# Gated delta rule and softplus MLP on one core: four of six base inverses in 32 lanes instead of two joined 16s, beta from SP and ACT, tile fills as scheduled items, another order

## The chip, the cores and the metric

The kernel runs on one core of one Trainium2 chip. The metric is the device time of one execution in microseconds. TensorE is called PE, VectorE DVE, ScalarE ACT, GpSimd POOL, and SyncE SP; SP, ACT and POOL issue the DMAs. DVE and POOL work on SBUF tiles of 128 partitions; results of PE lie in PSUM and are evicted by DVE or ACT.

## The reference

Two parts follow each other. The first is a gated delta rule over 4 batches, 8 heads, 768 positions and 48 features:

```python
k_n = k / (np.linalg.norm(k, axis=-1, keepdims=True) + 1e-06)
for t in range(S):
    y[:, :, t] = g[:, :, t] * einsum('bhd,bhde->bhe', q[:, :, t], state)
    v_old = einsum('bhde,bhd->bhe', state, k_n[:, :, t])
    state = state + beta[t] * einsum('bhd,bhe->bhde', k_n[:, :, t], v[:, :, t] - v_old)
```

The second takes y as a matrix of 3072 tokens by 384 features and computes `softplus(y @ w_in) @ w_out`, with 2048 hidden features.

## The kernel before

**Chunks and pairs.** The positions are cut into 12 chunks of 64. Within a chunk the recurrence is turned into matmuls; from chunk to chunk only the state is carried. Two chunks make a pair (pair 0 has chunks 0 and 1, pair 5 has chunks 10 and 11). Per chunk the kernel loads k, q, v and g (each in two DMAs of 192 KB, L249 and L271), scales k by its norm (L327 `kmul`, or a plain cast for pair 0), transposes k and q on PE (L345, L388), forms the products k k^T and k q^T (L503), evicts them (`kkc`; `mask`, L518), and runs the chain of the recurrence.

**The inverse of a pair.** Each chunk and head needs the inverse of a unit lower triangular matrix of 64 x 64, made of beta and k k^T. It is built in layers:

- The *base* is computed by DVE or POOL for all heads of both chunks at once: one partition holds one block. The strictly lower entries are transposed into lanes (L604 `kd1`, L611 `ln`), the tile `tt` is cleared (L619), its diagonal set to beta (L621), the entries scaled by beta into `nn` (L629 `prep`). Then `step` j, of two instructions (L639 a product into `tmp`, L646 an add into `tt`), adds row j's share to all rows below. Each partition holds two blocks of 16 x 16 (an upper and a lower one of a block of 32), so there are 15 steps.
- The two blocks of 16 are joined to one of 32, the *inner join*: `cv` (L228) and `tn` (L667, a transpose) bring the upper block back, `xmm` (L707, 32 matmuls a chunk) and `tmm` (L732, 32 a chunk) multiply it with the entries between the blocks, `xs` evicts between them and `thi` after them.
- `c16` casts `tt` to 16 bits, `t32` (L686) transposes it back, `tlo` writes it into `te` (used by `umm`, L855) and `to` (used by `zmm`, L770), scaled by masks.
- The outer join, from 32 to 64, is inside the recurrence: `zmm` and `z` (L779) make a tile z, and `zu` (L878) applies it.

nn, tt, tmp-like tiles have few buffers (nn 1, tt 1, tmp 2), so pairs follow each other there. Norms of pairs 2 to 5 take a power on POOL (`pow`, L566) after a square on ACT (L545) and a reduction on DVE (L549); pairs 0 and 1 take a square root on ACT.

**The chain of a chunk.** `ks` and `qs` (L813) multiply the state with k and q; `w` (L847) is v minus that; `umm`, the copy `u1`, `zu`, the copy `u2`; then `ymm` (L928) and `y` (L943, times g) give the output, and `smm` (L898) and `s` (L913) the next state. y is transposed (L962) into `xt`.

**The MLP** fills PE between: groups g1 (L992, into `h`, then softplus on ACT, L1004, into `ga`) and g2 (L1019, into `o`, copied by L218 or L220 and stored, L1039). A g1 group has 3 matmuls of 512 columns or 6 of 256, a g2 group 4 of 384. The weights come by eight DMAs from POOL (L297). `warm` items (L1064) are three matmuls on the identity whose result nobody reads.

**What sets the order.** Each piece of work is an item with the engines that may run it, the items it needs, and the buffers it uses. One list written into the kernel, `_ORDER`, names engine and number of every item: `P707` would put item 707 on PE. Engines work through their own part of the list in order, so an instruction that waits holds all behind it on its engine. A tile takes the first free buffer of its ring when its first item is emitted:

```python
for word in table.split():
    en, no = word[0], int(word[1:])
    it = self.items[no]
    ...
    for b in it.bufs:
        if b.ap is None:
            b.slot = b.ring.free.pop(0)
    it.fn(en)
```

Ahead of the list stand fixed instructions: identity, masks, the padding of kn and qn, the constant halves of the tiles te and z (L205, L212), and eight DMAs for beta from POOL (L175).

Of the kernel before, what the change touches and what calls it, by code (L numbers as in the profile page):

```python
# [74 lines left out]
def kernel(  # L75
# [20 lines left out]
    RAW = (0,)  # L96
    ON_ACT = (0, 1)
    IDLE = 24
# [34 lines left out]
    r_nv = ring("nv", 3, [P, 32], F32)  # L133
# [5 lines left out]
    r_mt = ring("mt", 10, [P, H, C], F16)  # L139
# [12 lines left out]
    r_w = ring("w16", 4, [P, H, D], F16)  # L152
# [15 lines left out]
    for r in range(2):  # L168
        for hf in range(2):
            l0 = 32 * (2 * r + hf)  # L170
            src = beta[2 * r : 2 * r + 2].rearrange(
                "p h (c l r) -> (p h) l c r", l=2, r=64
            )
            for cl in range(2):
                nc.gpsimd.dma_start(  # L175
                    out=beta_l[l0 + 16 * cl : l0 + 16 * cl + 16],
                    in_=src[:, cl, :, 32 * hf : 32 * hf + 32],
                )
# [25 lines left out]
    for t in r_te.tiles:  # L204
        nc.vector.tensor_copy(t[:, :, HC:], id64[:, 1, None, :].broadcast_to([P, U, HC]))  # L205
# [23 lines left out]

    def f16ps(ap):  # L230
        return ap.bitcast(F16)
# [6 lines left out]


# [296 lines left out]
    nv_of, td_of, z_of = {}, {}, {}  # L536
    root_last = [None]
# [38 lines left out]
    def inverse(cc, kk, kk_it, kkd, kd_it, nv, nv_it):  # L576
# [11 lines left out]
        if raw:  # L588
            bl_it = add("lbeta", tag, "D", lbeta, deps=[nv_it], bufs=[nv, nl, bl])
            bb = [bl]  # L590
        else:
            bl_it, bb = None, []
# [5 lines left out]
        if not raw:  # L598
# [4 lines left out]
            def kd1(en):  # L603
# [12 lines left out]
        en0 = "D" if first else "G"  # L616
        eng = ENG[en0]
        prev = add("clear", tag, "D" if first else "GD",
                   lambda en: ENG[en].memset(tt.ap, 0.0), bufs=[tt])  # L619
        prev = add("diag", tag, en0,  # L620
                   lambda en: eng.tensor_copy(  # L621
                       tt.ap.rearrange("p b i j -> p b (i j)")[:, :, ::17],
                       bl_ap().rearrange("p (b i) -> p b i", b=2),
                   ),
                   deps=[prev, bl_it], bufs=[tt] + bb)

        def prep(en, b):
            r = slice(16 * b, 16 * b + 16)
            eng.tensor_tensor(  # L629
                nn.ap[:, b].rearrange("p i (t e) -> p i t e", e=2),  # L630
                ln.ap[:, 8 * b : 8 * b + 8, r].rearrange("p t i e -> p i t e"),
                bl_ap()[:, r, None, None].broadcast_to([P, 16, 8, 2]),
                ALU.mult,
            )

        def step(en, j):
            n, w = 15 - j, j + 1
            t = tmp.ap[:, : 2 * n * w].rearrange("p (b i c) -> p b i c", b=2, c=w)
            eng.tensor_tensor(  # L639
                t,  # L640
                nn.ap[:, :, j + 1 :, j : j + 1].broadcast_to([P, 2, n, w]),
                tt.ap[:, :, j : j + 1, :w].broadcast_to([P, 2, n, w]),
                ALU.mult,
            )
            rows = tt.ap[:, :, j + 1 :, :w]
            eng.tensor_tensor(rows, rows, t, ALU.add)  # L646

        for b in range(2):
            prev = add("prep", f"{tag}.{b}", en0, lambda en, b=b: prep(en, b),
                       deps=[l1, prev, bl_it], bufs=[ln, nn] + bb)  # L650
        for j in range(15):
            prev = add("step", f"{tag}.{j}", en0, lambda en, j=j: step(en, j),
                       deps=[prev], bufs=[nn, tt, tmp], size=2 * (15 - j) * (j + 1))

        tw, tv, td, tn = Buf(r_tw), Buf(r_tv), Buf(r_td), Buf(r_tn)
# [517 lines left out]
```

## Time and profile before

| | |
|---|---|
| three runs | 254.86, 257.12, 260.44 us; median 257.12 |
| the profiled execution | 255.46 us, span 253.6 us, mean granted clock 0.966 |
| busy in the span | PE 93%, DVE 61%, ACT 60%, POOL 50% |
| costliest groups | softplus (L1004) 56.3 us, g1 (L992) 73.3, g2 (L1019) 70.3, POOL steps (L639, L646) 30.1 and 29.4, pow (L566) 21.8 |
| DMA | 27.56 MB in all, near 180 GB/s until 63 us |

The span is from the first to the last instruction of the profiled execution; the time has a little around it. Busy shares count an engine as busy while an instruction of its own is running; matmuls overlap, so PE's share is no measure of how well it is used. The page's digits show tenths of 40 equal slices of 6.34 us.

### The profile page before, as it was taken

Reading aid. Unit: us, or ns where it says so; the run is one execution under the profiler, and the core shown is the slowest. Engines: PE = TensorE matmul, PEld = TensorE weight load, DVE = VectorE, ACT = ScalarE, POOL = GpSimd, SP = SyncE. Lnnn points to the kernel's source line nnn. Section 1 sums busy time; section 2 is a strip of 40 time slices with the busy share of each in tenths; the row PEclk is TensorE's granted clock in tenths of the full one; section 3 lists DMA queues with packets and bytes.
Section 4 is the critical chain, followed back from the end, with each engine's and each line's share of the span. In section 5 each row is a group of like instructions: output and inputs, shape, how many; then the busy total and the mean of one; then the engine's idle time right before and its main releaser. Section 6 shows DMA issues by size and latency. Waiting matters only on the chain.

```text
span 253.6 us, 11355 instructions
## 1 busy us (share of the span) xinstructions
PE 236.9 (93%) x5040; PEld 160.5 (63%) x5040; DVE 153.7 (61%) x311; ACT 153.0 (60%) x285; POOL 127.1 (50%) x227
## 2 busy tenths in 40 slices
PE   7976588998989999999999999999999999999993
PEld 3543577676766765666766767755676565777751
DVE  7789888775893699759697588523843315313000
ACT  3557777686866579973777675456453475223530
POOL 8201653978879889988948859884000000000000
PEclk9999757799999999999999999999999999999999
DMA  8999999999990789083943850643024130112113
GB/s 111 198 181 178 178 179 180 186 195 176 176 153 6 173 180 157 4 200 83 156 98 84 170 99 22 124 83 80 3 66 93 23 80 0 34 32 48 34 47 78
DMA packets 86192, 27.56 MB, mean 109 GB/s; under 512 B 76288, under 2 KB 86144, under 8 KB 86144
## 3 DMA queue, kind: packets, MB, share of 16 engines
q1 hardware_dynamic: 80096, 23.21, 50.2%
q0 software_dynamic: 3968, 3.25, 8.2%
q10 hardware_dynamic: 2080, 0.39, 1.2%
q8 instruction: 39, 0.64, 1.2%
q14 instruction: 9, 0.07, 0.1%
HBM read 25.26 MB, written 4.72 MB: 118 GB/s over the span
## 4 chain that ended last, share of the span: by engine, by line
PE 76%; DVE 9%; DMA 4%; issue 3%; SPq 2%; ACT 2%; POOL 2%; ACTq 0%; DVEq 0%; POOLq 0%
PE h L992 25%; PE o L1019 23%; PE d L813 4%; DMA beta_l<-in_beta_dram 3%; PE d L855 3%; PE d L732 3%; PE d L770 3%; PE d L878 2%; PE d L928 2%; PE d L503 2%; PE d L707 2%; PE d L898 2%; PE d L388 2%; PE d L345 2%; POOL beta_l L175 2%
## 5 line engine op out<-in xcount | busy, mean ns | idle before, releaser
L1004 ACT ACTIVATE ga<-h 128x512 f16<-128x512 f32 x96 | 56.3, 598 | 33.4 <-PE h L992 27.6
L992 PE MATMUL h<-xt,w_in 128*128 128x512 f16 (+1 forms) x384 | 73.3, 330 | 0.1
L1019 PE MATMUL o<-w_out,ga 128*128 128x384 f16 x384 | 70.3, 326 | 1.4 <-issue 0.7
L1019 PEld LDWEIGHTS <-ga 128*128 128x128 f16 x384 | 35.7, 98 | 23.9 <-issue 1.8
L992 PEld LDWEIGHTS <-w_in 128*128 128x128 f16 x384 | 35.6, 99 | 20.7 <-issue 0.6
L639 POOL TENSOR_TENSOR tmp<-nn,tt 128x30 f32<-128x30 f32 (+7 forms) x75 | 30.1, 401 | 5.6
L646 POOL TENSOR_TENSOR tt<-tt,tmp 128x30 f32<-128x30 f32 (+7 forms) x75 | 29.4, 392 | 5.9
L566 POOL TENSOR_TENSOR nv<-nv,half_c 128x32 f32<-128x32 f32 x4 | 21.8, 5456 | 5.1 <-DVE nv L549 5.1
L218 ACT ACTIVATE kqt<-d 128x1024 f16<-128x1024 f16 (+1 forms) x21 | 18.4, 903 | 7.0 <-PE d L388 6.1
L218 ACT ACTIVATE osb<-o 128x384 f32<-128x384 f32 x18 | 8.8, 489 | 21.5 <-PE o L1019 21.4
L943 DVE TENSOR_TENSOR yg<-d,gf 128x384 f16<-128x384 f32 x24 | 12.8, 553 | 13.6 <-PE d L928 10.2
L1064 PE MATMUL o<-ident 128*128 128x512 f16 x72 | 19.3, 411 | 1.4 <-POOL ident masks.py:199 1.4
L847 DVE TENSOR_TENSOR w<-vf,d 128x384 f16<-128x384 f32 x22 | 11.3, 549 | 12.0 <-PE d L813 10.8
L218 ACT ACTIVATE u<-d 128x384 f16<-128x384 f32 x31 | 14.3, 491 | 7.1 <-PE d L878 3.3
L218 ACT ACTIVATE kk<-d 128x256 f16<-128x256 f32 (+1 forms) x34 | 12.8, 413 | 7.8 <-PE d L503 6.4
L518 DVE TENSOR_TENSOR mt<-d,mask 128x256 f16<-128x256 f32 x40 | 15.5, 418 | 3.2 <-PE d L503 1.9
L220 DVE CAST u<-d 128x384 f16<-128x384 f32 x17 | 9.1, 549 | 13.1 <-PE d L878 11.6
L813 PEld LDWEIGHTS <-kqt 48*64 48x64 f16 x704 | 13.3, 108 | 5.5 <-issue 5.3
L220 DVE COPY osb<-o 128x384 f32<-128x384 f32 x6 | 3.3, 556 | 21.6 <-PE o L1019 21.6
L813 PE MATMUL d<-s,kqt 48*64 48x48 f16 x704 | 16.4, 188 | 0.0
L545 ACT ACTIVATE ksq<-kf 128x768 f32<-128x768 f32 x12 | 10.1, 843 | 7.6 <-DMA kf<-in_k_dram 6.7
L220 POOL CAST tw<-tt 128x256 f16<-128x256 f32 x10 | 5.4, 563 | 16.1 <-DVE tt L646 16.0
(110 smaller groups left out, 380.1 us busy)
## 6 DMA issues: line engine op xcount, KB each, us to landing
qf<-in_q_dram SPq DMA_DIRECT2D x24, 192.0 KB, 5.1
vf<-in_v_dram SPq DMA_DIRECT2D x24, 192.0 KB, 5.2
gf<-in_g_dram SPq DMA_DIRECT2D x24, 192.0 KB, 4.2
out_dram<-osb SPq DMA_DIRECT2D x48, 96.0 KB, 2.4
kf<-in_k_dram SPq DMA_DIRECT2D x22, 192.0 KB, 5.1
w_in<-in_moe_w_in_dram POOLq DMA_DIRECT2D x4, 384.0 KB, 7.5
w_out<-in_moe_w_out_dram POOLq DMA_DIRECT2D x4, 384.0 KB, 12.9
kf<-in_k_dram ACTq DMA_DIRECT2D x2, 192.0 KB, 7.5
```

Of the source, the lines that this page charges most:

```text
L218: nc.scalar.activation(o, x, AF.Copy, scale=float(sign))
L220: ENG[en].tensor_copy(o, x)
L518: nc.vector.tensor_tensor(mt[c][m].ap[:, NP * p : NP * p + NP], gb[m].ap.rearrange("p (n b) -> p n b", n=NP)[:, :, C:], mask[:, None, :].b ...
L566: lambda en: nc.gpsimd.tensor_tensor(nv.ap, nv.ap, half_c, ALU.pow),
L639: eng.tensor_tensor(t, nn.ap[:, :, j + 1 :, j : j + 1].broadcast_to([P, 2, n, w]), tt.ap[:, :, j : j + 1, :w].broadcast_to([P, 2, n, w]), ...
L646: eng.tensor_tensor(rows, rows, t, ALU.add)
L813: nc.tensor.matmul(hd(o.ap)[HALF[r], NP * p + i], kq_of(c)[FEAT[m], 8 * p + 2 * i + r, off : off + C], s0[r].ap[FEAT[m], NP * p + i], **st ...
L943: lambda en, m=m: nc.vector.tensor_tensor(heads(yg.ap, m), hd(yp[m].ap), heads(gf.ap, m), ALU.mult),
L992: nc.tensor.matmul(hp.ap[:, n * b : n * b + n], w_in[:, j, f * P : (f + 1) * P], xt.ap[:, j, t0 : t0 + n], start=(j == 0), stop=(j == 2),)
L1004: lambda en, hp=hp, o=gb: nc.scalar.activation(o.ap, hp.ap, AF.Softplus),
L1019: nc.tensor.matmul(op.ap[:, :DM], b.ap[:, col + c0 : col + c0 + 128], w_out[:, f, :], start=(f == 0), stop=(f == NF - 1),)
L1064: nc.tensor.matmul(wb.ap.rearrange("p (a b) -> p a b", a=4), ident, ident[:, None, :].broadcast_to([P, 4, P]),)
```

## The change

- Pairs 2 to 5 (`WIDE`) compute their base in 32 lanes: one block of 32 x 32 a partition, 31 steps, `tt` and `nn` of 1,024 elements, `tmp` of up to 256. `cv`, `tn`, `xmm`, `xs`, `tmm` and `thi` fall away for them; `tlo` writes all 32 columns. Pairs 0 and 1 stay in two 16s.
- The steps of pairs 1 to 5 may now stand on DVE or POOL item by item (`en0`); the list alternates them inside a pair: of the wide steps 73 stand on DVE and 51 on POOL.
- beta is loaded by eight items, four on SP and four on ACT, instead of eight instructions on POOL ahead of the list.
- The constant halves of te and z are filled by items (`fte`, `fz`) on DVE, ACT and POOL.
- v of chunk 0 is scaled into w directly (`w0`), without the separate `vs`.
- There are 32 `warm` items instead of 24. Rings: nv 2 instead of 3, mt 9 instead of 10, w16 3 instead of 4, tmp 1 instead of 2.
- Five `gate` items on POOL copy one column each of kn, kk and kqt of chunks 0 and 1.
- `_ORDER` is another list, on all engines. Among others the SP list brings q of chunk 1 before that of chunk 0, and v3, k6 and k7 before g1; and POOL scales k of chunks 2 and 3.

The diff without the list, tile sizes and names cut where they repeat:

```diff
+    WIDE = (2, 3, 4, 5)
-    IDLE = 24
+    IDLE = 32
...
-    r_n = ring("nn", 1, [P, 2, 16, 16], F32)
-    r_tmp = ring("tmp", 2, [P, 128], F32)
-    r_t = ring("tt", 1, [P, 2, 16, 16], F32)
+    r_n = ring("nn", 1, [P, HC * HC], F32)
+    r_tmp = ring("tmp", 1, [P, HC * HC // 4], F32)
+    r_t = ring("tt", 1, [P, HC * HC], F32)
...
-            for cl in range(2):
-                nc.gpsimd.dma_start(
-                    out=beta_l[l0 + 16 * cl : l0 + 16 * cl + 16],
-                    in_=src[:, cl, :, 32 * hf : 32 * hf + 32],
-                )
...
-    for t in r_te.tiles:
-        nc.vector.tensor_copy(t[:, :, HC:], id64[:, 1, None, :].broadcast_to([P, U, HC]))
-    for t in r_z.tiles:
-        nc.vector.tensor_copy(t[:, :, :HC], pat[:, None, :].broadcast_to([P, 16, HC]))
+    fill_te = [add("fte", f"f{i}", "DAG", ...) for i, t in enumerate(r_te.tiles)]
+    fill_z = [add("fz", f"f{i}", "DAG", ...) for i, t in enumerate(r_z.tiles)]
...
+                def beta_load(en, r=r, hf=hf, cl=cl):
+                    l0 = 32 * (2 * r + hf) + 16 * cl
+                    src = beta[2 * r, 0, C * cl + 32 * hf :]
+                    ENG[en].dma_start(out=beta_l[l0 : l0 + 16], in_=bass.AP(...))
+                beta_it.append(add("beta", f"{r}{hf}{cl}", "SA", beta_load))
...
-        en0 = "D" if first else "G"
-        eng = ENG[en0]
+        en0 = "D" if first else "DG"
+        wide = cc in WIDE
+        nb, bs = (1, HC) if wide else (2, HC // 2)
...
         def step(en, j):
-            n, w = 15 - j, j + 1
-            t = tmp.ap[:, : 2 * n * w].rearrange("p (b i c) -> p b i c", b=2, c=w)
-            eng.tensor_tensor(
+            n, w = bs - 1 - j, j + 1
+            t = tmp.ap[:, : nb * n * w].rearrange("p (b i c) -> p b i c", b=nb, c=w)
+            nn_, tt_ = n_ap(), t_ap()
+            ENG[en].tensor_tensor(
...
-        for j in range(15):
+        for j in range(bs - 1):
...
-        cv = add("cv", tag, "DG", cvs, deps=[prev], bufs=[tt, tv])
+        cv = None if wide else add("cv", tag, "DG", cvs, deps=[prev], bufs=[tt, tv])
...
-        for cl in range(2):
+        for cl in () if wide else range(2):
             xp = Buf(p_d)
...
-                        en, b.ap[:, :, :16], td.ap[:, :, :16], own[:, x : x + 1]
+                        en, b.ap[:, :, :bs], td.ap[:, :, :bs], own[:, x : x + 1]
...
-            its = [
+            its = lo if wide else [
...
-                a2 = add("w0", f"{c}.{m}", "DGA",
-                         lambda en, m=m, w1=w1: copy(en, w1.ap, heads(vf.ap, m)),
+                a2 = add("w0", f"{c}.{m}", "DG",
+                         lambda en, m=m, w1=w1: ENG[en].tensor_tensor(w1.ap, heads(vf.ap, m), ..., ALU.mult),
...
+    gates = pool.tile([P, 8], F16, name="gates")
+    for x, (it, b) in enumerate(gate_of):
+        add("gate", f"{x}", "G", ..., deps=[it], bufs=[b])
```

More of the change, by code (lines that the diff above doesn't have):

```diff
@@ L228, in scaled @@
             ENG[en].tensor_scalar_mul(o, x, by)
+    fill_te = [
+        add("fte", f"f{i}", "DAG",
+            lambda en, t=t: copy(
+                en, t[:, :, HC:], id64[:, 1, None, :].broadcast_to([P, U, HC])
+            ))
+        for i, t in enumerate(r_te.tiles)
+    ]
+    fill_z = [
+        add("fz", f"f{i}", "DAG",
+            lambda en, t=t: copy(en, t[:, :, :HC], pat[:, None, :].broadcast_to([P, 16, HC])))
+        for i, t in enumerate(r_z.tiles)
+    ]
     def f16ps(ap):
@@ L588, in inverse @@
         if raw:
[L589 removed]
+            bl_it = add("lbeta", tag, "D", lbeta, deps=[nv_it] + beta_it, bufs=[nv, nl, bl])
             bb = [bl]
@@ L820, in chain @@
         vs = None
-        if cc in RAW:
+        if cc in RAW and not first:
             vs = add("vs", f"{c}", "GD",
```

251 lines of the change are left out of this document (145 added, 106 removed).

## The prediction

> **What bounds the kernel now.** I read the page first, then windows, chain, timeline, rows by form, DMA. From the page:
>
> ```profile
> span 253.6 us, 11355 instructions
> PE 236.9 (93%) x5040; PEld 160.5 (63%) x5040; DVE 153.7 (61%) x311; ACT 153.0 (60%) x285; POOL 127.1 (50%) x227
> PE   7976588998989999999999999999999999999993
> DVE  7789888775893699759697588523843315313000
> POOL 8201653978879889988948859884000000000000
> PEclk9999757799999999999999999999999999999999
> ```
>
> From slice 10 (63 us) TensorE is never free, while POOL, which computes the base inverses, is done after slice 28 (178 us). Two windows, and three pieces of the chain of waits (start, length, x matmuls):
>
> ```profile
> 27.90:41.50 13.60, 11.78 (x325) 10.69 (x321) 10.88 (x21) 10.79 (x24) 9.27 (x10) 0.50 1.08 185
> 60.00:249.00 189.00, 187.28 (x4000) 126.38 (x3998) 105.51 (x188) 113.46 (x210) 95.66 (x177) 1.00 0.45 88
> ```
>
> ```profile
> 56.16 0.65 PE o L1064 x3
> 98.00 1.11 PE d L707 x64
> 191.54 0.91 PE d L732 x58
> ```
>
> In the windows the first pair of numbers after the length is PE's busy time: 187.3 of 189 us from 60 to 249, so there any work taken from PE shows in the end, as long as nothing else falls behind. The page's PEclk dips in slices 5 to 8; the first window shows the granted clock 0.50.
>
> How early the inverses are ready is in the timeline: POOL ends the last one (pair 5, chunks 10 and 11) at 173.8, and PE's L770 needs it for chunk 10 at 199.0 and for chunk 11 only at 218.3.
>
> ```profile
> 164.06 0.43 POOL L639 TENSOR_TENSOR tmp<-nn,tt 128x128 f32<-128x128 f32 x1
> 164.56 0.45 POOL L646 TENSOR_TENSOR tt<-tt,tmp 128x128 f32<-128x128 f32 x1
> 170.47 0.24 POOL L639 TENSOR_TENSOR tmp<-nn,tt 128x30 f32<-128x30 f32 x1
> 172.92 0.84 POOL L220 CAST tw<-tt 128x256 f16<-128x256 f32 x2
> 218.27 0.66 PE L770 MATMUL d<-to,kk 64*64 64x32 f16 x32
> ```
>
> **The change, part by part.** *PE.* Pairs 2 to 5 lose L707 and L732: 4 x (1.11 + 1.0) = 8.4 us (58 of 64 of L732 took 0.91). Eight more fills of three 512-column matmuls (L1064) at 0.65 each come back: 5.2. Both lie in dense stretches, the fills at the first three chunks, so I count the net: -3.2 us. If every added fill lay in a PE gap it would be -8.4, if half the removed work was hidden, +1.
>
> *The base inverses.* In 16 lanes a pair takes 15 steps of two instructions over 1,360 elements each way; in 32 lanes 31 steps over 5,456. Rows by form:
>
> ```profile
> L629 POOL TENSOR_TENSOR nn<-ln,beta_l 128x256 f32<-128x256 f16 x10 | 6.0, 619 | 4.6 <-DVE ln L611 3.3 <-DVE nv L570 1.3
> L639 DVE TENSOR_TENSOR tmp<-nn,tt 128x30 f32<-128x30 f32 x2 | 0.4, 197 | 0.1
> L639 DVE TENSOR_TENSOR tmp<-nn,tt 128x126 f32<-128x126 f32 x2 | 0.6, 292 | 0.1
> L629 DVE TENSOR_TENSOR nn<-ln,bl 128x256 f32<-128x256 f16 x2 | 0.8, 422 | 0.0
> L566 POOL TENSOR_TENSOR nv<-nv,half_c 128x32 f32<-128x32 f32 x4 | 21.8, 5456 | 5.1 <-DVE nv L549 5.1
> ```
>
> DVE: 168 ns + 1.0 per element (30, 126 and 256 elements), and 42 between dependent ones. POOL: 190 + 1.9 per element (0.24 for 30, 0.44 for 128; the 256 of L629 at 619 would give 1.7), and 78 between (164.06 + 0.43 to 164.56). The built order puts 73 of the 124 wide steps on DVE, 51 on POOL, alternating inside each pair. They are one chain: each step reads the last, and nn, tt and tmp have one buffer, so pair k+1 begins when pair k is cast.
>
> The chain, from the end of the second step of pair 2 (time S) to the matmul L770 of chunk 11:
> - POOL: 102 x 0.268 + 18,290 x 0.0019 = 62.1
> - DVE: 71 steps, 142 x 0.210 + 25,358 x 0.0010, = 55.2
> - three times clear (1.0), diag (0.2) and prep of 1,024 elements (1.2; the last on POOL 1.9): 7.9; four casts: 5.0 (POOL's two of 256 take 0.84; 1,024 in one on DVE or ACT lie between 1.0 and 1.9, I take 1.0 to 1.1, POOL 1.9)
> - one pow (L566) stands on POOL between two steps of pair 2: 5.4
> - transpose and the two scalings te, to after the last cast: 2.3
>
> That is 138. At each change of pair DVE first has other work: the transpose (1.03), ln (1.05), two w (0.55 each), a copy of o, and a pow that is not fully covered, some 8 in all. Elsewhere POOL's runs (1 to 9.7 us) are as long as what DVE does beside them, so I add nothing. Sum 146; bounds 138 to 156.
>
> *Port.* Beside DVE's wide operation a POOL step can stand still:
>
> ```profile
> 64.85 1.44 DVE L604 SCALAR_TENSOR_TENSOR kkd<-kk,own,kkd 128x1024 f16<-128x1024 f16 x1 [0.98 <-ACT kkd L226]
> 65.29 1.19 POOL L639 TENSOR_TENSOR tmp<-nn,tt 128x78 f32<-128x78 f32 x1
> ```
>
> The next of the same size takes 0.34: 0.85 lost. Two such a pair would cost 7; DVE's wait beside may swallow them; I take 1. [...]
>
> *When S is.* Beta leaves POOL (L175, 4.5 us of issue) for SP and ACT, four each at some 0.7 us; the fills lie before data arrives. This trace has no beta from SP or ACT: the last is issued at about 7, and at the 2.4 to 5.1 us from issue to landing of the page's groups it lands between 9.5 and 12; DVE needs it at 12.3. That saves the 0.8 idle at L585 (0.3 if another 0.5 us passes). The transpose tn ahead of a reduction saves 0.9. So the first pair is 1.6 earlier. But pair 1 waits for POOL, whose queue is now: two k-scalings (1.5 each), the cast of q4, three weight issues (0.8), pow (5.4), a weight issue, prep (1.2), nine steps (8.1).
>
> ```profile
> q1 hardware_dynamic: 80096, 23.21, 50.2%
> q0 software_dynamic: 3968, 3.25, 8.2%
> ```
>
> 50.2% of the span for 23.21 MB is 1.08 us for a 192 KB load, and 8.2% 2.6 us per weight. The second half of q4 is the 28th load: 28 x 1.08 + 2 weights + 2 us start + some 1.5 in which SP waits for a q buffer = 39. Then 0.8 + 2.4 + 5.4 + 0.8 + 1.2 + 8.1 + 1 (POOL's first two steps took 0.84 and 0.86) = 58.7, DVE's six steps to 62. Cast, reduction, y, tn, clear, L604, ln, prep, two steps and three masks follow on DVE: 10. S = 72; 66 if q4 is no brake, 76 if other loads are (below).
>
> *Sum.* S 72 + chain 146 + port 1 = 219 at L770 of chunk 11. PE would get there at about 210: in the new order 179 us of its work lie before it, and 31 us of gaps as in this trace (249 less 217.5 of work at the dense rates 0.65 per group and 0.2 to 0.5 for the small ones). So PE waits some 9 us, spread over the pairs, the 3.2 are lost and 6 more. Behind that point PE has 35 (28 groups L1019, 16 L992 at 0.65, the last two chunks' small ones), a gap of 0.6 as at 246.65 in the timeline, and 4.2 from the last matmul to the end (249.4 to 253.6): 259 to 260. ACT loses some 10 us of evictions off the path; nothing. The gates are five one-column POOL copies; nothing, covered by POOL's waits.
>
> Profiled time is 255.46 for a span of 253.6; 259.5 gives 261.4, +2.3%. The median of the three runs, 257.12, is 0.65% above the profiled one; on that scale 263, and I say **262**.
>
> **Rivals.** (1) PE stays the bound: not slower. If POOL's runs hide DVE's other work and S is 66 to 68, the chain reaches 210 with PE; then only -3.2 counts: span 250.5, 254 on the scale of the median. For it: DVE was free for 2.3 of each 10 us from 30 to 160; against: it gains 56 us of steps and loses some 16 (four tn, five thi, nine copies u, two k-scalings). It decides when S + chain falls under 210. (2) The added fills keep the clock at 1.0 where it was 0.50 (27.9 to 41.5) and the first pair's gain reaches chunk 1: PE regains up to 5 of 11.8, S 62: span 246, 249. Against: the small matmuls there wait for ACT and DVE. (3) Loads come late: the new SP order puts g1 41st, behind k6, k7 and v3 (here 33rd). 41 x 1.08 + 6 weights x 2.6 + 3.5 = 63.4, needed at 64; y of chunk 1 stands before tn on DVE and the reduction's square of k7 before u of chunk 1 on ACT. At 1.25 us a load it is 70, S 78: span 265, 269.
>
> **Chances.** Chain as forecast 0.44 (own range 256 to 268), (1) 0.27, (2) 0.11, (3) 0.18. About 2% is what a measurement of this kernel can tell from no change: its three runs spread over 2.2%. Faster: (2) and a part 0.06 of (1), 0.17. Same: the rest of (1) and 0.14 of the forecast, 0.35. Slower: 0.48. The range takes in (1) and (3): 250 to 273.
>
> **What would show it.** Right: POOL busy until about 215 instead of 174; 62 steps a pair at 0.19 + 1.9 per element; idle PE before L770 and L855 of chunks 4, 6, 8 and 10, 1 to 4 us each; ACT or PE waiting on te and to. S is the second wide step of pair 2 on DVE: 66 or 78 tells (1) from (3). Wrong: PE without gaps from 75 on, or the clock at 1.0 from 28 to 48, or the last cast of pair 5 before 205.

## The result, and the profile after

The changed kernel takes **274.77 us** (median of four runs, 273.24 to 276.14) beside 256.96 for the kernel before: 1.072 times, 95% interval 1.061 to 1.083. It is slower by 7%; the forecast was 262, and 274.8 lies 1.8 us above its range. The profiled execution took 273.24 us for a span of 271.5; the four executions have spans of 271.5 to 274.4, so a single span says nothing about differences of 1 or 2 us. Executions that took clearly longer than the fastest of their kernel (260.44 us of the kernel before, beside 254.86) are left out of all ratios, and as the profile of run e3 fell on one (289.12 us, the fastest 283.71), e3 has a ratio alone.

From the page of the changed kernel:

```profile
span 271.5 us, 10475 instructions
PE 241.9 (89%) x4552; PEld 156.2 (58%) x4552; DVE 193.6 (71%) x446; ACT 163.2 (60%) x290; POOL 117.4 (43%) x168
...
PE   6468686959999999989997999989799999999993
...
DVE  5578869757998879889788998798958664624100
...
POOL 6200646983774665646642858160562412000000
PEclk9858996688999999999999999999999999999999
```

DVE is up by 40 us of busy time, TensorE dips in slices 21 and 28 (counted from 0) and is thin until slice 8, and POOL works until slice 33. Three answers of the timeline show the second wide step of pair 2 (its end is S), the last step and the cast of pair 5, and the matmuls of z that use them:

```profile
78.64 0.22 DVE L661 TENSOR_TENSOR tmp<-nn,tt 128x60 f32<-128x60 f32 x1
78.89 0.22 DVE L668 TENSOR_TENSOR tt<-tt,tmp 128x60 f32<-128x60 f32 x1
...
224.14 0.25 POOL L668 TENSOR_TENSOR tt<-tt,tmp 128x31 f32<-128x31 f32 x1
224.46 1.26 POOL L205 CAST tn<-tt 128x1024 f16<-128x1024 f32 x1
...
229.40 0.68 PE L801 MATMUL d<-to,kk 64*64 64x32 f16 x32
```

S is 79.1 (forecast 72), L801 of chunk 11 (L770 before) comes at 229.4 (219), and 42.1 us follow to the end (40). L801 shows no idle time in front of it: its tile `to` was ready at 227.3, and TensorE was at dense groups until 229.4.

A fixed point helps to see where the time went: the start of the first matmul of L738 for chunk 2 (L707 before), when pair 1's inverse, the last in 16 lanes, reaches TensorE. I call it T2: 70.5 before, 73.5 after. The windows split at T2, first the kernel before, then the changed one (after the stretch and its length come busy time and count of PE, PEld, DVE, ACT and POOL, then the granted clock, the DMA share and GB/s):

```profile
0.00:70.50 70.50, 59.57 (x1188) 41.62 (x1189) 56.39 (x138) 47.66 (x92) 40.26 (x72) 0.88 1.09 176
70.50:253.60 183.10, 177.35 (x3852) 118.93 (x3851) 97.27 (x174) 105.31 (x194) 86.82 (x156) 1.00 0.42 83
```

```profile
0.00:73.50 73.50, 55.15 (x1076) 35.22 (x1076) 54.03 (x140) 47.34 (x87) 36.36 (x56) 0.84 1.01 166
73.50:271.50 198.00, 186.73 (x3477) 121.02 (x3476) 139.59 (x307) 115.88 (x203) 81.00 (x113) 1.00 0.42 77
```

The same windows for the dense groups alone, L992 before and L1032 after:

```profile
0.00:70.50 70.50, 13.46 (x96) 9.45 (x96) 0.88 1.09 176
```

```profile
0.00:73.50 73.50, 9.43 (x48) 5.55 (x48) 0.84 1.01 166
```

Six matmuls make a group there: 16 groups before T2 became 8, and 4 groups of L1019 became none of L1059. For a ledger, count each of TensorE's items at its length at full clock (0.65 for a dense group or a fill, 0.2 to 0.5 for the small ones, as in the prediction) and call the rest gaps; a gap is then either TensorE standing still or a matmul that took longer than at full clock:

| us | before | after | difference |
|---|---|---|---|
| to T2: work + fills + gaps | 33.0 + 15.5 + 22.0 | 24.0 + 16.8 + 32.6 | +3.0 |
| behind T2: work + fills + gaps | 169.0 + 0 + 9.9 | 169.9 + 3.9 + 19.7 | +14.5 |
| from the last matmul to the end | 4.2 | 4.6 | +0.4 |

TensorE lost 8.1 us of work, as the change says (202.0 to 193.9), and gained 5.2 of fills. But its gaps grew by 20.4 us: 10.6 before T2, where twelve dense groups (7.8 us) are no longer done and have to follow later, and 9.8 behind it. By the windows' busy times TensorE stands still for 18.4 us before T2 instead of 10.9 and, from T2 to its last matmul, for 6.7 instead of 1.6; the rest of the gaps is longer matmuls (the clock before T2 is 0.84 instead of 0.88).

### The profile page after: what moved, and what is told of

Read it like the earlier page. It is cut to its first block, busy times and chain, and to the rows that moved or that the text cites. A ratio compares the mean times of both kernels' runs of the same rounds, so it can differ in the third digit from the quotient of the medians.

```text
span 271.5 us, 10475 instructions
## 1 busy us (share of the span) xinstructions
PE 241.9 (89%) x4552; PEld 156.2 (58%) x4552; DVE 193.6 (71%) x446; ACT 163.2 (60%) x290; POOL 117.4 (43%) x168
## 4 chain that ended last, share of the span: by engine, by line
PE 29%; DVE 25%; POOL 24%; DMA 10%; issue 6%; ACT 2%; SPq 2%; ACTq 0%; POOLq 0%; DVEq 0%
PE o L1059 12%; PE h L1032 10%; DVE tmp L661 9%; DVE tt L668 9%; POOL tt L668 8%; POOL tmp L661 8%; DMA kf<-in_k_dram 4%; POOL nv L582 4%; DMA qf<-in_q_dram 4%; DMA beta_l<-in_beta_dram 2%; DVE nn L650 2%; PE d L846 2%; DVE td L717 1%; PE d L895 1%; SPq L264 1%
## 5 line engine op out<-in xcount | busy, mean ns | idle before, releaser
L1032 PE MATMUL h<-xt,w_in 128*128 128x512 f16 (+1 forms) x384 | 76.0, 338 | 0.7 <-DMA w_in<-in_moe_w_in_dram 0.4
L1044 ACT ACTIVATE ga<-h 128x512 f16<-128x512 f32 x96 | 56.5, 598 | 33.3 <-PE h L1032 31.4
L1059 PE MATMUL o<-w_out,ga 128*128 128x384 f16 x384 | 70.8, 327 | 0.6 <-ACT osb L203 0.6
L661 POOL TENSOR_TENSOR tmp<-nn,tt 128x192 f32<-128x192 f32 (+23 forms) x60 | 32.8, 547 | 57.6 <-DVE tt L668 52.4
L1032 PEld LDWEIGHTS <-w_in 128*128 128x128 f16 x384 | 36.0, 101 | 22.3 <-issue 0.8
L1059 PEld LDWEIGHTS <-ga 128*128 128x128 f16 x384 | 35.3, 98 | 23.1 <-issue 0.8
L661 DVE TENSOR_TENSOR tmp<-nn,tt 128x30 f32<-128x30 f32 (+19 forms) x94 | 30.0, 320 | 15.6 <-POOL tt L668 12.9
L668 POOL TENSOR_TENSOR tt<-tt,tmp 128x192 f32<-128x192 f32 (+23 forms) x60 | 33.7, 562 | 4.7
L668 DVE TENSOR_TENSOR tt<-tt,tmp 128x30 f32<-128x30 f32 (+19 forms) x94 | 30.2, 321 | 3.2
L1114 PE MATMUL o<-ident 128*128 128x512 f16 x96 | 26.7, 415 | 1.4 <-POOL ident masks.py:199 1.4
L203 ACT ACTIVATE u<-d 128x384 f16<-128x384 f32 x40 | 18.5, 491 | 12.5 <-PE d L918 8.5
L203 ACT ACTIVATE kqt<-d 128x1024 f16<-128x1024 f16 (+1 forms) x23 | 20.7, 916 | 3.4 <-PE d L360 1.9
L533 DVE TENSOR_TENSOR mt<-d,mask 128x256 f16<-128x256 f32 x40 | 15.8, 415 | 0.5 <-ACT kk L203 0.5
L1114 PEld LDWEIGHTS <-ident 128*128 128x128 f16 x96 | 8.9, 105 | 10.8 <-issue 3.7
L518 PE MATMUL d<-kqt 48*64 48x128 f16 x320 | 9.4, 231 | 5.8 <-ACT kqt L203 3.3
```

Source lines behind the costliest of these rows:

```text
L203: nc.scalar.activation(o, x, AF.Copy, scale=float(sign))
L533: nc.vector.tensor_tensor(mt[c][m].ap[:, NP * p : NP * p + NP], gb[m].ap.rearrange("p (n b) -> p n b", n=NP)[:, :, C:], mask[:, None, :].b ...
L661: ENG[en].tensor_tensor(t, nn_[:, :, j + 1 :, j : j + 1].broadcast_to([P, nb, n, w]), tt_[:, :, j : j + 1, :w].broadcast_to([P, nb, n, w]) ...
L668: ENG[en].tensor_tensor(rows, rows, t, ALU.add)
L1032: nc.tensor.matmul(hp.ap[:, n * b : n * b + n], w_in[:, j, f * P : (f + 1) * P], xt.ap[:, j, t0 : t0 + n], start=(j == 0), stop=(j == 2),)
L1044: lambda en, hp=hp, o=gb: nc.scalar.activation(o.ap, hp.ap, AF.Softplus),
```

## The experiments

All are edits of the changed kernel except a1, b1, b2 and b3, which are edits of the kernel before. "Behind" is the span less T2. Ratios are to the kernel before, run on the same chip, with 95% intervals. The intervals of c2, e6, e1, e5, e9 and e11 overlap that of the changed kernel; for these the reading rests on single lines of the traces more than on the time.

| run | what is edited | ratio | span | T2 | behind |
|---|---|---|---|---|---|
| before | | 1 | 253.6 | 70.5 | 183.1 |
| after | the change | 1.072 (1.061 to 1.083) | 271.5 | 73.5 | 198.0 |
| e4 | short wide steps | 1.038 (1.030 to 1.046) | 263.3 | 72.6 | 190.7 |
| c2 | no power on POOL | 1.069 (1.063 to 1.075) | 270.3 | 73.2 | 197.1 |
| e6 | twelve fills out | 1.075 (1.066 to 1.083) | 273.5 | 73.0 | 200.5 |
| e7 | dense groups early | 1.104 (1.093 to 1.115) | 281.2 | 79.8 | 201.4 |
| e8 | e7 and short steps | 1.074 (1.065 to 1.084) | 273.4 | 79.5 | 193.9 |
| e1 | beta from POOL | 1.060 (1.052 to 1.068) | 270.1 | 72.4 | 197.7 |
| e5 | square of k6 later | 1.067 (1.057 to 1.078) | 273.3 | 73.7 | 199.6 |
| e9 | order of loads | 1.062 (1.055 to 1.069) | 268.6 | 70.4 | 198.2 |
| e10 | e9 and dense early | 1.094 (1.087 to 1.101) | 276.3 | 76.0 | 200.3 |
| e11 | e9 and beta from POOL | 1.080 (1.075 to 1.086) | 273.7 | 74.8 | 198.9 |
| e2 | 16 lanes again | 1.128 (1.119 to 1.138) | 286.1 | 74.3 | 211.8 |
| e3 | e2 and beta from POOL | 1.115 (1.102 to 1.127) | | | |
| a1 | beta from SP and ACT | 1.011 (1.005 to 1.017) | 254.9 | 72.8 | 182.1 |
| b1 | pair 5 wide, POOL and DVE | 1.029 (1.023 to 1.035) | 261.5 | 70.2 | 191.3 |
| b2 | pair 5 wide, POOL | 1.004 (1.000 to 1.008) | 253.7 | 70.5 | 183.2 |
| b3 | b2, te earlier | 0.996 (0.993 to 1.000) | 252.1 | 70.5 | 181.6 |

The line that orders the table: with the wide steps of all four pairs at full length "behind" is 197 to 201 us, whether T2 is 70.4 or 79.8. What an edit does to T2 shows at the end, with 1 to 4 us of scatter.

### The length of the wide chain: e4 and c2

```diff
-            n, w = bs - 1 - j, j + 1
+            n, w = bs - 1 - j, (j + 8) // 8 if wide else j + 1
```

> The changed kernel with the steps of the wide pairs shortened: each of the 124 steps still issues its two instructions on its own engine, but on an eighth of the columns, so the inverses of pairs 2 to 5 are left unfinished. By the rows of the steps the chain behind S falls from 149 to about 85. Theory (the length of the chain is what TensorE waits for after 80): L770's counterpart for chunk 11 is served by 170, TensorE's gaps after 85 us shrink from 18.6 to 5 to 8, span 214.6 of work + 32 + 5 to 8 = 252 to 256, time 254 to 258, 0.99 to 1.005. Rival (the loss is the early stage and the loads; the wide steps run beside TensorE's work): gaps stay, 268 to 274, 1.045 to 1.07.

The time fell, to 1.038 and a span of 263.3, but not to 252 to 256. From 85 to 249 TensorE is now never free; the same window of the changed kernel follows:

```profile
85.00:249.00 164.00, 163.88 (x3125) 105.89 (x3123) 105.49 (x280) 103.54 (x184) 43.37 (x101) 1.00 0.44 82
```

```profile
85.00:249.00 164.00, 158.17 (x3058) 101.45 (x3052) 125.43 (x277) 102.02 (x180) 72.83 (x103) 1.00 0.44 82
```

By the ledger 7.4 of the 9.8 us of new gaps behind T2 go. So the wide steps hold TensorE back, at a price of some 8 us; the other 9.7 us over the kernel before are there without them. Neither theory held alone. Nor did the chain shrink as expected: the steps' busy time fell from 108.7 to 56.5 us, but L801 of chunk 11 came at 221.2, not at 170, only 8.2 earlier, because the order ties the steps to TensorE's other work.

```diff
-  lambda en: nc.gpsimd.tensor_tensor(nv.ap, nv.ap, half_c, ALU.pow)
+  lambda en: nc.gpsimd.tensor_tensor(nv.ap, nv.ap, half_c, ALU.mult)
```

> The changed kernel with the power on POOL (L582, four times 5.6 us, the root of the norms of pairs 2 to 5) replaced by a product of the same shape, so that the norms are left without their root. Theory (two of the four stand between wide steps in the chain behind S, one stands ahead of the steps of pair 1): S falls by 2 to 4 us, the chain behind it from 150 to 139 to 141, and the time falls until TensorE's own work is the bound, as with the short steps (span 263): span 258 to 262, 1.015 to 1.035. Rival (the power fills time in which POOL would wait for DVE or for loads): S as before and the chain shorter by 0 to 5, span 266 to 271.

The rival was right: S 78.9, span 1.2 us shorter, although the chain of waits of the changed kernel names the power twice between wide steps (105.83 and 150.63, 5.4 us each). What POOL waits for says why; first the changed kernel, then c2, between 80 and 230 (waiting engine, tile and line, for whom: us in total, times, longest):

```profile
POOL tmp L661 <- DVE tt L668: 51.1, 16, 6.5
...
POOL kn L342 <- DVE nv L588: 2.1, 1, 2.1
...
POOL tmp L661 <- DVE nn L650: 1.8, 1, 1.8
```

```profile
POOL tmp L661 <- DVE tt L668: 51.1, 16, 6.5
...
POOL tmp L661 <- DVE nn L650: 6.8, 1, 6.8
POOL kn L342 <- DVE nv L588: 6.6, 1, 6.6
```

POOL waits 51 us for DVE's steps either way, and two other waits for DVE grow by 4.5 and 5.0 us, 9.5 together, about what the two powers took. DVE runs what POOL waits for between other work that hangs on TensorE and ACT, so time taken from POOL comes back as waiting. The chain is not a sum of its own durations; TensorE's 174 us of work behind T2 are woven into it.

### Fills and dense groups: e6, e7, e8

```diff
-    IDLE = 32
+    IDLE = 20
 # _ORDER: warm 3.x, 4.x, 5.x (67 to 83 us) out
```

> The changed kernel without the twelve fills that it runs between 67 and 83 us (groups 3, 4 and 5 of L1114, 12 x 0.65 = 7.8 us of TensorE); 20 of 32 fills are left, all else stands. Theory (there TensorE has nothing else that is ready: it waits for pair 1's inverse and for chunk 1, and what follows hangs on the chain from S): S stays at 78 to 79, the fills' time turns into gaps, and the time falls by 0 to 2 us, 1.06 to 1.07. Rival (the fills stand in TensorE's queue ahead of work that is ready, and of what DVE and POOL wait for): the time falls by 5 to 8 us, 1.04 to 1.05. If TensorE's clock falls where the fills were, that shows in the granted clock between 67 and 90.

Nearest to the theory: S is 79.4 and the time does not fall. It does not fall even a little (1.075, where 1.06 to 1.07 was expected), because the fills' time did not turn into gaps alone. Granted clock between 67 and 90, first e6, then the changed kernel (the third number from the end):

```profile
67.00:90.00 23.00, 17.30 (x362) 13.86 (x363) 19.89 (x47) 13.25 (x23) 13.81 (x15) 0.55 0.75 126
```

```profile
67.00:90.00 23.00, 22.73 (x532) 15.01 (x528) 21.39 (x50) 17.05 (x31) 13.67 (x15) 1.00 0.68 112
```

Without the fills the clock is 0.55 there, and TensorE does 134 fewer other matmuls in the same 23 us (362, against 532 less the 36 of the fills): what the fills took is lost to slower matmuls.

```diff
 # _ORDER, on top of e6
+G wload w0.3, w1.1, w0.1 ahead of cast q4;  G wload w1.0, w1.2, w1.3 ahead of pow 4
+P g1:0.0 and the eight g2:0.* in the fills' places;  A o:0.0, o:0.1 behind them
```

> As the kernel without the twelve fills, and in their places the eight groups of L1059 of chunk 0 (and the last of L1032 of chunk 0), which the changed kernel runs from 84 to 103; for that the six later weight issues on POOL move up, three ahead of the cast of q4 (which waited 5.6 us for its load) and three ahead of the power of pair 2. The kernel before had 16 groups of L1032 and 4 of L1059 done at 70 us, the changed one 7 and none. Theory (two bounds in tandem: TensorE's own work is 10 us late by 70, and the chain from S is late too): TensorE gets ahead by 5 to 8 us at 100, but waits for the chain later: the gaps after 85 grow, and the time falls by 1 to 4 us against the changed kernel, 1.05 to 1.065. Rival (the late dense work is the whole loss, the chain only looks binding because TensorE comes late): the time falls by 9 or more, below 1.035.

> The last edit and the shortened wide steps together (each step on an eighth of its columns, so that the inverses of pairs 2 to 5 are left unfinished). The shortened steps alone gave a span of 263.3. Theory of two bounds: with both relieved the time falls below either alone, to a span of 254 to 257, 1.00 to 1.015 of the kernel before. Rival (the dense work that comes early is only moved, TensorE waits as long elsewhere before 85): span 261 to 264, as with the shortened steps alone.

Both missed: e7 is slower by 9.7 us of span, e8 by 10.1 than e4. T2 moved to 79.8 and 79.5. Between 40 and 60, e7 shows:

```profile
DVE vf L856 <- DMA vf<-in_v_dram: 7.1, 1, 7.1
```

The weights had gone ahead of v1 in the transfers, and DVE stood for v1 with everything behind it. (Both kernels also lack the twelve fills, and their pages have the clock at 0.5 in slices 4 to 8: 28 to 63 us in e7, 27 to 62 in e8.) Even with the short steps the loss came through whole: behind T2, e8 is within 3.2 us of e4.

### The early stage: a1, e1, e9, e5, e11, e10

The listing of the changed kernel as built shows what ACT's issues of beta wait for (DMAHW0 to 7 are eight counters, and in the trace each goes up when a DMA of SP or ACT lands):

```
L264 DMACopy kf_71<-in_k_dram
L203 Activation te_121<-id_204
L203 Activation z_124<-pat
L246 DMACopy beta_l<-in_beta_dram [waits DMAHW5]
L203 Activation te_120<-id_204
L561 Activation ksq_88<-kf_70 [waits DMAHW1,DMAHW0]
L246 DMACopy beta_l<-in_beta_dram [waits DMAHW7]
```

The DMAs of SP and ACT share these eight in turn here, and an issue waits until the DMA that had its counter before has landed: ACT's issues at 8.61 and 9.88 begin 0.02 us after two loads that SP issued at 3.22 and 4.50 land, at 8.59 and 9.86, and of the 108 issues for which the trace has that landing none ends before it. Eight DMAs more are a whole turn. ACT's timeline after the change, 8 to 11 us:

```profile
8.61 0.63 ACTq L246 DMA_DIRECT2D beta_l<-in_beta_dram  x1
9.29 1.06 ACT L203 ACTIVATE te<-id 128x1024 f16<-128x1024 f16 x1 [3.89 <-DMA beta_l<-in_beta_dram]
9.88 0.60 ACTq L246 DMA_DIRECT2D beta_l<-in_beta_dram  x1
10.25 0.83 ACT L561 ACTIVATE ksq<-kf 128x768 f32<-128x768 f32 x1
```

The square of k0 starts at 10.25 instead of 5.89; a fill of te, 1.06 us long, also stands in front of it. Run a1 makes this part alone in the kernel before:

```diff
-            nc.gpsimd.dma_start(out=beta_l[...], in_=src[...])   # eight, ahead of the list
+            beta_it.append(add("beta", f"{r}{hf}{cl}", "SA", beta_load))
```

> The kernel before with the beta part alone: eight DMAs from SP and ACT in the places that they have in the changed kernel, none from POOL. My prediction had this at 0.8 us earlier for the first pair. Theory (in the program as built all DMAs of SP and ACT take eight semaphores in turn, and an issue waits until the DMA eight before it has landed, so eight small DMAs use up a whole turn): ACT's square and cast of k0 and k1 stand behind beta issues, the first step of pair 0 starts at 17 to 19 instead of 15.56, q2 and q0 land 1 to 2 us later; the inverses have slack in this kernel, so the time is 1.00 to 1.01. Rival (beta's landing is what counts, POOL's setup gains 4.5 us): first step at 14.5 to 15.5, time 0.99 to 1.00.

Its timeline, and the same step of the kernel before:

```profile
17.89 0.20 DVE L645 TENSOR_TENSOR tmp<-nn,tt 128x30 f32<-128x30 f32 x1
```

```profile
15.56 0.20 DVE L639 TENSOR_TENSOR tmp<-nn,tt 128x30 f32<-128x30 f32 x1
```

The first pair starts 2.3 us later, T2 is 2.3 later, and the time is 1.011. The theory held; its price was a little above the range. Here the square of k0 is not late (5.61): ACT stands 4.2 us with three issues of beta between it and the cast of k0, and the square of k1 starts at 11.10 instead of 9.38. In the changed kernel the part is undone by e1 (the same diff backwards):

> The changed kernel with one part undone: beta comes again from POOL, by the eight DMAs of the kernel before, ahead of the mask; the eight items on SP and ACT are gone, the rest of the order stands. Theory (the early stage was upset by the new beta issues: they stand in the queues of ACT and SP, ACT's next instruction waited 3.9 us for one, the reduction of k0 came at 11.1 instead of 6.8 and the last beta landed after 15): the reduction of k0 starts before 8, the first step of pair 0 starts at 15 to 16 instead of 18.4, and S (end of the second wide step of pair 2 on DVE) falls from 79 to 74 to 76; the chain behind S stays near 149, so the time falls by 3 to 5 us, to about 1.055 of the kernel before. Rival 1 (the late k6, which holds ACT's square and then TensorE from 55.9 to 59.3, sets S whatever the first pair does): first step at 15 to 16, but S still 78 to 80 and the time within 1 us of the changed kernel, 1.07. Rival 2 (beta is not what delays the first pair; the fills as items on ACT are): first step still at 18 or later.

Less than expected: the first step starts at 15.8, so beta is what delays the first pair, and the pair reaches TensorE 2.5 us earlier (26.3 against 28.8). But of that 1.1 are left at T2, and 1.1 at S (78.0, where 74 to 76 was expected). There other waits end last. Between 40 and 66 in the changed kernel:

```profile
POOL qn L205 <- DMA qf<-in_q_dram: 5.6, 1, 5.6
ACT ksq L561 <- DMA kf<-in_k_dram: 4.0, 1, 4.0
...
PE d L518 <- ACT kqt L203: 2.9, 1, 2.9
```

```diff
 # e9, SP's part of _ORDER
+load q4.1 behind q4.0, q5.1 behind q5.0, v1.0 behind v1.1;  v3.0, v3.1 behind v2;  q7.1 beside q7.0
```

> The changed kernel with SP's order of loads alone altered: the second halves of q4, q5 and v1 follow their first halves (in the changed kernel they come 5, 6 and 9 loads later; q4 landed at 41.5 and v1 at 43.7, in the kernel before at 31.4 and 26), and v3 and the first half of q7, landed at 42 to 58, go back behind v2 and beside the other half of q7 (in the kernel before 65 to 71). Theory (the order of the loads makes the stage up to 80 us late: POOL stood 5.6 us for q4, and the weights, the power and the steps of pair 1 stand behind that): POOL's wait falls below 1 us, the third part of w_in lands before 45 instead of 49, S falls from 79 to 75 to 77, the time by 2 to 4 us, 1.055 to 1.06. Rival (the power of pair 2 waits for the square of k5 in any case, and TensorE for the steps): S 78 to 79 and the time within 1 us.

POOL's cast no longer waits, S is 76.6 and the span 2.9 shorter, as expected; the ratio, 1.062, and the third part of w_in, at 45.8, lie just outside. T2 is 70.4, that of the kernel before, and still the span is 15 us longer.

```diff
 # e5
-A ksq:6 ahead of kev q5, k4;  D red:6 ahead of step 9 of pair 1
+A ksq:6 behind kev k4;        D red:6 behind step 11
```

> The changed kernel with one item of ACT and one of DVE moved: the square of k6 stands behind kev of q5 and k4 on ACT, and its reduction behind step 11 of pair 1 on DVE. In the changed kernel that square waited 4.0 us for k6 (landed at about 55), and TensorE then waited 2.9 us for kev of k4 behind it, with DVE's masks and steps 9 to 14 behind that. Theory (this late load is part of what makes S late): the 2.9 us are gone, S falls from 79 to 76 to 77 and, the chain behind S being the same, the time falls by 2 to 3 us, to 1.06 of the kernel before. Rival (S is set by POOL, whose steps of pair 1 end at 63.5 in any case, and by what DVE has to do after them): S 78 to 79, time within 1 us.

The rival's numbers came: TensorE's 2.9 us wait is gone, S is 79.3. Its reason was only half of it: DVE now takes up step 9 at 63.7 instead of 66.1, but then stands 1.65 us for TensorE's matmuls of y (L968), and the gain is gone.

> The same order of loads and beta from POOL ahead of the mask, as in the kernel before; the wide inverses and all fills as in the changed kernel. Theory (each us of S shows at the end): S 73 to 75, time 266 to 268, 1.04 to 1.045; it does not come under 1.03 however early the loads are, since from S = 72 on the chain of 149 and the 43 behind it give 264. Rival (what beta saved alone, 1.4 us of span, and what the loads save are the same waiting and do not add): 1.055 to 1.06.

> The same order of loads, and on top of it the edit of the dense groups (weights up in POOL's order, eight groups of L1059 of chunk 0 in the places of the twelve fills between 67 and 83, which are gone). By itself that edit made the changed kernel 8 us slower than without the fills: three weights ahead of v1 and k6 made v1 land at 54.6 instead of 43.7, and DVE stood 7.1 us for it. Theory (the DMA queue is full from 20 to 65, and what counts is which transfers are first in it): with v1, q4 and q5 first, the weights can be early too; TensorE's work without fills reaches 24 to 28 us at 70 (22.3 in the changed kernel, 33.0 in the kernel before), S 75 to 77, time 266 to 270, 1.035 to 1.055. Rival (early weights cost the k loads as much as they bring): no faster than with the loads' order alone, 1.06 to 1.08.

Both missed. In e11 (e9 with e1) S is 81.2. Its waits from 28 to 70:

```profile
POOL nv L578 <- DVE nv L561: 13.2, 1, 13.2
...
ACT ksq L557 <- DMA kf<-in_k_dram: 9.7, 2, 6.3
```

With beta out of the way POOL issued the three weights at 35.6 to 37.9, in e9 at 39.4 to 41.7. ACT's squares then stood for their loads (6.3 us the longest), DVE stood 10.6 us for the squares instead of 2.1, and the power behind k5's began at 51.1 instead of 46.6. In e10 (e9 with e7) a square waited 7.3 us in the same way. The page's DMA digits are 9 from slice 3 to 9 of the changed kernel (20 to 68 us): in e7, e10 and e11 issues brought forward there went with later loads elsewhere, and edits that helped alone did not add.

### Undoing the wide lanes: e2, e3

```diff
-    WIDE = (2, 3, 4, 5)
+    WIDE = ()
 # _ORDER: steps 15 to 30 out; cv, tn, xmm, xs, tmm, thi of pairs 2 to 5 in, behind step 14
```

> The changed kernel with the other part undone: WIDE is empty, so pairs 2 to 5 are again inverted in 16 lanes with the inner join (64 matmuls and two reductions and scalings per pair); beta, fills and order stand, the join's items are put behind the last step of each pair. Theory (the chain of wide steps that begins at S = 79 is what holds TensorE back after 80 us, the early stage only shifts it): the gaps of TensorE after 85 us (18.6 us in the changed kernel) shrink to 5 to 8, its work grows by 8.4 to 223, the gap up to 82 us stays at about 32; span 260 to 264, time 262 to 266, 1.02 to 1.035 of the kernel before. Rival (the late early stage is passed on to TensorE by itself, through k, q and the weights, with the inverses waiting for nothing): TensorE's gaps after 85 us stay above 14, and with 8.4 us more work the time is 278 to 283, 1.08 to 1.10.

> Both parts undone together: 16 lanes with the inner join, and beta from POOL; what is left of the change are the fills as items (eight more of TensorE's, those of the padded tiles), the gates and the order. Theory: the two parts are not independent. Without the wide chain an early stage that is 3 us earlier helps only where TensorE waits for it before 82 us, so this is 1 to 4 us under the kernel with 16 lanes alone: 258 to 264, 1.00 to 1.03. Rival (the order itself is the loss: loads and weights in it come too late whatever beta does): above 1.03.

Inconclusive. I put the join's items in by hand; in e2 TensorE stood 3.4 us at 90 to 94 for tn, behind cv on POOL, behind a power that waited 13.5 us for a load. That prices my placing, not 16 lanes.

### A wide pair where the chain has slack: b1, b2, b3

```diff
+    WIDE = (5,)
 # b1: steps 0 to 14 on POOL, 15 to 30 on DVE between its items; tlo (to) on ACT ahead of o of chunk 6
 # b2: all steps on POOL; c16, t32 on DVE behind s of chunk 9; tlo (to) behind o; zmm:10 ahead of z:10
 # b3: as b2, tlo (te) behind w of chunk 10, zmm:10 four groups earlier
```

> The kernel before with one pair alone made wide: pair 5 (chunks 10 and 11) in 32 lanes without the inner join, its first 15 steps on POOL as before and its last 16 on DVE, one or two after each of DVE's items from s of chunk 8 on; all else is the order of the kernel before (one buffer fewer for w and for nv, to make room). Theory (wide steps cost nothing where the chain has slack: the kernel before finished pair 5 on POOL at 173.8, and TensorE needed it at 199 and 218): POOL ends its part at about 177, DVE at about 196, TensorE loses no time and saves the 64 matmuls of the join twice, 2.1 us: 0.99 to 0.995 of the kernel before. Rival (DVE's steps stand in the way of w, u and z of chunks 8 and 9 and TensorE waits for those): 1.00 to 1.02.

> The kernel before with pair 5 alone in 32 lanes, this time all its 31 steps on POOL (which is free after 173.8 there), its cast and transpose on DVE behind s of chunk 9, the scaling to on ACT behind an eviction of chunk 8 rather than ahead of one, and the matmuls of z of chunk 10 nine groups later. In the first try POOL's part and DVE's part ended where they should (176.8 and 195.3), but to stood 5.6 us in ACT's queue ahead of an eviction that TensorE needed. Theory (with slack in the chain and nothing put ahead of other work, the join's matmuls saved are a gain): POOL ends its steps at 196 to 197, TensorE has no gap over 1 us between 180 and 205, and the time is 0.99 to 0.997 of the kernel before. Rival (the wide pair ends just too late for chunk 10 whatever engine it is on): 1.00 to 1.01, with TensorE waiting for to or te at 198 to 203.

> The kernel before with pair 5 alone wide, all on POOL, as in the last try, with te scaled on DVE directly behind w of chunk 10 (ahead of z) and the matmuls of z of chunk 10 four groups earlier. Theory (the join's 2.1 us saved show as soon as nothing waits): the wait of 1.3 us for te goes, span 252 to 253, 0.99 to 1.000 of the kernel before. Rival (what TensorE does not wait for here it waits for later, since chunk 10's recurrence follows chunk 9's at the speed of DVE and ACT): 1.000 to 1.006.

In b1 both engines ended where expected (176.8 and 195.3), yet 8 us were lost. One item in the wrong place took part in it:

```profile
197.12 1.15 ACT L227 ACTIVATE to<-td,own 128x1024 f16<-128x1024 f16 x1 [5.64 <-DVE td L704]
198.18 0.47 ACT L219 ACTIVATE osb<-o 128x384 f32<-128x384 f32 x1
```

TensorE waited 3.7 us for the eviction at 198.18, which stood behind the scaling. With that and other placements changed b2 is level with the kernel before, and b3 is 0.4% faster (interval 0.05% to 0.7%), the only version whose interval lies below 1. Behind T2 it saves 1.5 us while POOL works 20 us more:

```profile
70.50:252.10 181.60, 175.64 (x3725) 116.91 (x3724) 96.29 (x173) 103.53 (x189) 106.34 (x183) 1.00 0.43 83
```

## Why the prediction was wrong, step by step

**PE, right in size.** -8.4 for the join and +5.2 for fills gave -3.2; the ledger has -8.1 and +5.2. That fills in dense stretches cost their whole length was not borne out: e6 shows that taking twelve away brings nothing.

**The cost of a step, right.** POOL's 102 wide instructions were to take 62.1 with 78 ns between them, so 54.1 without; DVE's 142, 49.2. The windows of L661 and L668 behind 78 us (DVE, whose 73 steps here take in the two ahead of S, then POOL):

```profile
78.00:271.50 193.50, 24.78 (x73) 28.75 (x51) 1.00 0.42 78
...
78.00:271.50 193.50, 24.88 (x73) 30.28 (x51) 1.00 0.42 78
```

DVE 49.7; POOL 59.0, of which about 5 are eight instructions that stood still beside others of their shape. One of them, between 178 and 182, with what DVE did beside it:

```profile
178.90 0.61 POOL L661 TENSOR_TENSOR tmp<-nn,tt 128x240 f32<-128x240 f32 x1
178.96 1.64 DVE L620 SCALAR_TENSOR_TENSOR kkd<-kk,own,kkd 128x1024 f16<-128x1024 f16 x1
179.59 1.55 POOL L668 TENSOR_TENSOR tt<-tt,tmp 128x240 f32<-128x240 f32 x1
```

The usual lengths are 0.61, 1.28 and 0.69. The term for such stalls, *Port*, was 1 in the sum, 7 at most, an estimate from one stall of 0.85; it was mis-sized by some 4. Seven of the eight stand beside L620 (L604 before, the one in the prediction's row) or a k-scaling (L342, L327 before), and wherever one of these began beside POOL's wide steps, the step that began next stood 0.6 to 0.9 us. Where POOL had begun 0.05 or 0.06 us before, DVE's instruction is longer too: L620 at 178.96 (1.64 for 1.28) and L342 at 127.01 (1.36 for 0.95). What makes them stand is not shown, and no run takes these instructions away to test it. POOL's 1.9 ns per element is borne out: steps of 240 elements without a stall took 0.61 and 0.69, which is 1.8 and 2.1 ns per element over 190 ns.

**The chain, right in size, wrong in kind.** 147 with *Port* was forecast from S to L801 of chunk 11, 150.3 measured (bounds 138 to 156 and 7), of which the last 2.1 are TensorE's own work. But I read it as a sum with slack for TensorE beside it, at whose end TensorE waits for the inverse. e4 took 52 us of steps out of it and gained 8, c2 took out 22 us of power and gained 1, so it was no such sum. And TensorE hardly waits for the inverses. Of the idle time of 1 to 4 us forecast before L801 and L895 of every wide pair, one piece came, 1.5 us before L895 at 193.5, for w on DVE. The longest one is elsewhere:

```profile
145.25 0.36 DVE L668 TENSOR_TENSOR tt<-tt,tmp 128x192 f32<-128x192 f32 x1
145.52 0.55 DVE L983 TENSOR_TENSOR yg<-d,gf 128x384 f16<-128x384 f32 x1
146.13 0.51 PE L1002 MATMUL d<-ident,yg 128*128 128x128 f16 x6 [1.74 <-DVE yg L983]
```

The matmuls of this y were done at 143.6, and y stood in DVE's queue behind six instructions of steps. So at least part of the steps' price is paid by DVE's other work, which comes late in its queue.

**When S is, wrong: the largest miss.** 72 forecast, 79.1 measured, beyond the 78 of rival (3). DVE's 10 us at its end were right (9.7); what failed is when the steps of pair 1 end, 69.4 instead of 62. POOL ended its nine steps at 63.7 instead of 58.7; the cast of q4, which heads that row, started at 42.9, when its load was in, instead of 39. DVE, held by the late square of k6 and masks, took up step 9 only at 66.1 (e5 gives that back, and loses it again to a wait for TensorE). The term "the first pair is 1.6 earlier" has the wrong sign: the first step is 2.8 later (18.38 instead of 15.56), and a1 gives 2.3 for beta alone. I had bounded beta by its issue and landing times, and never asked what the issues themselves wait for. Of the 7.1 us, e1 takes back 1.1 and e9 2.5; the rest stays open. In the forecast's own sum S is 7.1 of the 12 us that the span is too long; the chain adds 3.3 and the stretch behind it 2.

**"PE would get there at about 210", wrong.** The 179 us of work ahead of that point are right (179.5). The "31 us of gaps as in this trace" were 50, 10.6 of the difference before T2. I took TensorE's gaps from the old order, though the list of the changed kernel showed dense groups and the weights moved: weights were issued until 81.00 instead of 49.73. This also sank rival (1): with the steps cut to an eighth and TensorE never free from 85 to 249 the span is 263.3 (e4), not 250.5. The forecast's two bounds were both late through the same early stage, so neither could save the other, and a range built from S alone was too narrow.

**Rivals.** Of (2) the clock came and the gain did not. The clock is 1.00 where it was 0.50 (27.9 to 41.5), which the prediction also named as a sign of being wrong, but 0.50 from 11.8 to 22 and from 42.6 to 52.8, and the first pair is late. That the fills did it is not shown: in e4, with the same fills, the page has it at 0.5 to 0.6 in slices 5 to 7 (33 to 53 us). (The dip of the page before lies in slices 4 to 7, counted from 0, not 5 to 8.) (3) was right in kind and wrong in its loads: g1 landed near the forecast (the last of it at 65.2, not 63.4) and held nobody; q4 and k6 did. e9 prices the order of the loads at 2.9 us of span.

**Of the 17.9 us of span**, then: -8.1 work saved, +5.2 fills, +10.6 gaps before T2, +9.8 gaps behind it, +0.4 at the end. Of the gaps behind, 7.4 go with short steps (shown by e4). Of those before T2, beta (1.1) and the loads (3.1) take part; that the rest is dense work missing because weights come late is argued from the windows and the issues, and not shown: both tries to bring it back (e7, e10) ran into the transfers. Whether the wide lanes for all four pairs could pay with an early stage like that of the kernel before was not tried.

## What to carry to other kernels

Before pricing a chain, look what the new order does to the bound engine's work ahead of it: the 31 us of gaps carried over from the old order were 50 in the new one. A moved DMA cost here its issue (0.59 to 0.86 us for one of beta), its place among the transfers (DVE stood 7.1 us for v1 in e7), and its turn of the shared counters (3.9 us in front of ACT's fill of te), on the engine that issues it. Longer work on a side engine was free here in the one pair that has slack (b3: 20 us more of POOL, ratio 0.996; no other pair was tried alone), and there with no item that waits for it ahead of other work in the queue of its engine (b1 had one, which waited 5.64 us). On an engine with other duties, look also for what stands behind such work in its queue.

## What was not expected of the hardware

A chain of waits can name a 5.4 us instruction twice, and removing it gain 1.2 us (c2). Twelve fills that compute nothing were worth about what they cost, through the clock (0.55 without, 1.00 with, between 67 and 90). And eight DMAs of 12 KB on the queues of SP and ACT made the kernel before 1.1% slower (a1; 0.5% to 1.7%), where POOL's issue of them, 4.5 us long, had made DVE wait 0.8 us.
